# Seeding the fifth product's bank with the common term, in a kernel that sums a long convolution and a feed-forward block

## The chip, the cores and the metric

The kernel runs on one core of a Trainium2 chip. The metric is the device time of one execution in microseconds; several executions are timed and the median is given. A core has five engines that run their own instruction streams and wait for one another through semaphores: TensorE (PE; its weight loads are listed as PEld), VectorE (DVE), ScalarE (ACT), GpSimd (POOL) and SyncE (SP, which here only issues transfers). Matmuls write PSUM, eight banks of 128 partitions x 512 float32; VectorE and ScalarE move results from there.

## The reference

```python
def _A_ref(q, k, v, shift_k, ssm_k, ssm_D):          # S = 2048 tokens, D = 576 channels
    ...                                              # k_shift: causal depthwise conv of k, 4 taps
    kv = k_shift * v
    ...                                              # y: causal depthwise conv of kv with ssm_k, length 2048, by FFT
    y = y + kv * ssm_D[None, None, :]
    return q * y

def _B_ref(x, w1, w2):                               # w1 is 576 x 4608, w2 is 4608 x 576
    h = jnp.einsum("bsd,df->bsf", x, w1)
    h = jnp.maximum(h, zero)
    return jnp.einsum("bsf,fd->bsd", h, w2)

x = A_q
xn = _layernorm(x, axis=-1)
return x + _A_ref(xn, A_k, A_v, A_shift_k, A_ssm_k, A_ssm_D) + _B_ref(xn, B_w1, B_w2)
```

All numbers are float32. The first part (the convolution) and the second part (the feed-forward block) are independent until the last sum.

## The kernel before

**Split operands.** To keep float32 accuracy at the rate of the rounded type (fp32r), every matmul operand is split into a high part (a ScalarE copy) and a low part (the rest). A product of two operands is three matmuls: high x high, high x low, low x high.

**The feed-forward block.** The 2048 tokens go in two halves of 1024, and each half in two blocks of 512 (`b0`, `b1`). The 4608 hidden columns go in 18 chunks of 256, that is two tiles of 128 (`f` = 0, 1). So there are 36 pairs of a half and a chunk, numbered `g`. The first three (`PLAIN`) run plainly (`classical`, line 597). The other 33 run in `quad` (line 629). There the 2 x 2 arrangement of token blocks and of hidden tiles, with the contraction of 512 channels halved too, is multiplied with seven products in place of eight (the scheme of Strassen and Winograd). The sums of operands stand ready: `s1` to `s4` of the tokens, `sums` of the weights. The last 64 channels are added by `rest` (line 583): 2 matmuls. A `product` (line 574) is 6 matmuls of 512 columns: two contraction chunks of three.

**The banks of a quad.** Two PSUM banks carry the hidden results. `bank` (line 560) gives the two alternately, so a new bank waits until every reader of the one before it in the same place is done. In the order of the code, one quad does:

1. Bank 1 (`x`) gets the product of `wa` and `00`. ScalarE copies it, negated, into bank 2 (`y`, line 649). `x` then gets the product with `01` and the rest: it is the first result (block 0, tile 0).
2. `y` gets the product of `wb` and `s2`. It now holds the (negated) common term of the two other results. ScalarE copies it to SBUF (`u2`, line 664).
3. Bank 5 (`x` again) starts anew with the product of `wc` and `s1`. ScalarE copies that to SBUF (`p5`, line 670).
4. `y` gets the product of `wb` and `s3`; bank 5 gets the rest of block 0 and the product of `wd` and `s4`. VectorE adds `u2` to it (line 685): this is the second row's result (block 0, tile 1).
5. ScalarE copies `y`, negated, into bank 4 (line 687). `y` gets the rest of block 1, and VectorE adds `p5` (line 692): block 1, tile 1.
6. Bank 4 gets the product of `wc` and `11` and the rest: block 1, tile 0.

Each result goes through `hidden` (line 588). ScalarE takes the relu (`hh`, line 592) and VectorE the low part (`ll`, line 594).

**The second layer.** Between the products stand eight units of the quad before (`mm2`, line 725; in `quad` they are the calls `unit(0)` to `unit(7)`). A unit is one token tile of 128: 12 matmuls of 288 columns into a pair of banks. VectorE adds the pair to the accumulator (`acc`, line 751). In one stage of the convolution two units a quad are seeded with the accumulator by ScalarE (line 723) and copied back by ScalarE (line 744).

**The weights.** ScalarE makes the high part of a weight (line 513) and GpSimd the low part (line 514), from tiles that GpSimd's queue loads (lines 495 to 506). VectorE makes the sums of the weights (line 526).

**The convolution.** It is a Python generator, `conv` (line 783), whose steps are issued between the matmuls of the feed-forward block. After each product, rest and unit the code calls `tick` (line 1179) with the cost of what was just issued. `tick` issues up to two steps of the generator as long as the convolution lags behind its share. A step that needs a wide bank on loan (it yields "wide") is issued only where `place` is true. In a product, `tick` is called after the first three matmuls and after all six, and only the second call may place a wide step. The stages are: the other half's operands, the filter's transform (lines 916 to 931), taps, gate and transform of the input (lines 936 to 982), products of the spectra with a join and the way back (lines 1041 to 1076), and the last transform with the gate by `x` (lines 1123 to 1167).

**What sets the order.** All matmuls are chained in the order of the code (`tc.issue_after(done["pe"].ins)`). On the other engines, a planner orders instructions by modelled times (`schedule_with_timeline_sim=True`, line 1311). It is bound by data, by `issue_after` and, where both are ready, by the order of the code. The steps of the convolution stand behind the last accumulator addition on VectorE and behind the last relu or copy-back on ScalarE (`here`, line 254), and weight splits on ScalarE behind the latter too.

Of the kernel before, what the change touches and what calls it, by code (L numbers as in the profile page):

```python
# [10 lines left out]
F32 = mybir.dt.float32  # L11
F32R = mybir.dt.float32r
AF = mybir.ActivationFunctionType
OP = mybir.AluOpType
# [3 lines left out]
P = 128  # L18
# [28 lines left out]
W_MM = 512  # L47
# [52 lines left out]
def h3_ffn_kernel(ctx: ExitStack, tc, x, k, v, shift_k, ssm_k, ssm_D, w1, w2, fwd, inv, mid, out):  # L100
    nc = tc.nc
    x = x[0].rearrange("(p u t) d -> u p t d", u=U, t=T)
# [6 lines left out]
    hp = ctx.enter_context(tc.tile_pool(name="hp", bufs=2))  # L109
# [279 lines left out]
    def need(g, o):  # L389
        while g == PLAIN and o not in ready:  # L390
            post(1)
# [95 lines left out]
    raw1, raw2, wa, wb, wc, wd, wr, w2s, sums_w = ({} for _ in range(9))  # L487
# [56 lines left out]
    def split_c(g):  # L544
        wc[g] = split_sums(g, "wc", slice(2, 4))
# [14 lines left out]
    def bank(g, which, name):  # L560
        banks[g, name] = ps_h.tile([P, 512], F32, tag=f"h{(which + 1 + max(g - PLAIN, 0)) % 2}",
                                   name=f"psh{g}_{name}")
        return banks[g, name]

    def matmuls(ps, seq, start):


        for n, (a, m) in enumerate(seq):
            with tc.issue_after(done["pe"].ins) if "pe" in done and not n else nullcontext():
                last = nc.tensor.matmul(ps, a, m, start=start and n == 0, stop=n == len(seq) - 1,  # L570
                                        skip_group_check=True)
        done["pe"] = last

    def product(ps, w, off, o, start=False, g=None, place=True):

        need(g, o)
        for c in range(2):
            h, l = w[:, 0, off + c, :], w[:, 1, off + c, :]
            hi, lo = xo[o][:, 0, c, :], xo[o][:, 1, c, :]
            matmuls(ps, ((h, hi), (h, lo), (l, hi)), start and c == 0)  # L580
            tick(3 * W_MM, place and c == 1)

    def rest(ps, g, b, f):
        need(g, b)
        matmuls(ps, [(wr[g][:, n, 0, f * P:(f + 1) * P], hl[b]) for n in range(2)], False)
        tick(2 * W_MM)

    def hidden(g, b, f, ps):
        k = dict(bufs=2 - (b or f))
        hh = hp.tile([P, 512], F32R, tag=f"hh{b}{f}", name=f"hh{g}_{b}_{f}", **k)  # L590
        ll = hp.tile([P, 512], F32R, tag=f"ll{b}{f}", name=f"ll{g}_{b}_{f}", **k)
        done["act"] = nc.scalar.activation(hh, ps, AF.Relu)  # L592
        with tc.issue_after(done["centred"].ins):
            nc.vector.scalar_tensor_tensor(ll, ps, 0.0, hh, op0=OP.max, op1=OP.subtract)  # L594
        hid[g, b, f] = (hh, ll)
# [33 lines left out]
    def quad(g, units):  # L629


        def unit(n):
            if n + 1 < len(units):
                open_unit(*units[n + 1], n + 1 in stage["seeded"] and more)
            mm2(*units[n])
            post(1)

        def later(o):
            if g == NQ - 1:
                (load_operand if isinstance(o, str) else load_rest_operand)(o)  # L640

        b0, b1 = (0, 1) if g < NQ else (2, 3)
        more = g + 1 < QUADS
        x = bank(g, 0, "1")
        y = bank(g, 1, "2")
        open_unit(*units[0])
        product(x, wa[g], 0, "00", start=True, g=g, place=False)
        later("00")
        nc.scalar.activation(y, x, AF.Copy, scale=-1.0)  # L649
        unit(0)  # L650
        split_c(g)
        unit(1)
        product(x, wa[g], 2, "01", g=g)
        later("01")
        rest(x, g, b0, 0)
        hidden(g, 0, 0, x)
        unit(2)
        split_w2(g, 0)
        if more:
            load_w2(g + 1, 0)  # L660
        product(y, wb[g], 0, "s2", g=g)
        later("s2")
        u2 = hp.tile([P, 512], F32, tag="u2", name=f"u2_{g}", bufs=1)
        nc.scalar.activation(u2, y, AF.Copy)
        unit(3)
        x = bank(g, 0, "5")
        product(x, wc[g], 2, "s1", start=True, g=g)
        later("s1")
        p5 = hp.tile([P, 512], F32, tag="p5", name=f"p5_{g}", bufs=1)
        nc.scalar.activation(p5, x, AF.Copy)  # L670
        if more:
            split_a(g + 1)
        unit(4)
        product(y, wb[g], 2, "s3", g=g)
        later("s3")
        if more:
            sums(g + 1)
        split_w2(g, 1)
        if more:
            load_w2(g + 1, 1)  # L680
        rest(x, g, b0, 1)
        later(2)
        product(x, wd[g], 0, "s4", g=g, place=False)
        later("s4")
        nc.vector.tensor_tensor(u2, x, u2, OP.add)  # L685
        x = bank(g, 0, "4")
        nc.scalar.activation(x, y, AF.Copy, scale=-1.0)  # L687
        hidden(g, 0, 1, u2)
        unit(5)
        unit(6)  # L690
        rest(y, g, b1, 1)
        nc.vector.tensor_tensor(p5, y, p5, OP.add)  # L692
        hidden(g, 1, 1, p5)
        if more:
            split_b(g + 1)
            split_d(g + 1)
            split_r(g + 1)
            if g + 2 < QUADS:
                load_w1(g + 2)
        unit(7)  # L700
        product(x, wc[g], 0, "11", g=g)
        later("11")
        rest(x, g, b1, 0)
        later(3)
        hidden(g, 1, 0, x)

    def token(g, b, i):
        return (g // NQ) * HT + b * BT + i
# [6 lines left out]
    def open_unit(g, b, i, seed=False):  # L715

        t = token(g, b, i)
        slot["open"] = 1 - slot["open"]
        ps = ps_o.tile([P, 2, 512], F32, tag=f"o{slot['open']}", name=f"pso{g}_{t}")
        open_ps[g, t] = ps, slot["open"]  # L720
        if seed and slot["open"] not in unwritten:
            seeded.add(t)
            nc.scalar.activation(ps[:, :, :NH], two(acc[t]), AF.Copy)

    def mm2(g, b, i):
        t = token(g, b, i)
        end = g == QUADS - 1
        if end:
            while t not in added:
                next(stream)  # L730
        cols = slice(i * P, (i + 1) * P)
        ps, slot["closed"] = open_ps.pop((g, t))
        unwritten.discard(slot["closed"])
        slot["units"] += 1
        for h in range(2):
            dc = slice(h * NH, (h + 1) * NH)
            seq = []
            for f in range(FT):
                hh, ll = hid[g, b, f]
                for a, m in ((hh, 0), (hh, 1), (ll, 0)):  # L740
                    seq.append((a[:, cols], w2s[g, f][:, m, dc]))
            matmuls(ps[:, h, :NH], seq, t not in seeded)
        if t in seeded:
            done["act"] = nc.scalar.activation(two(acc[t]), ps[:, :, :NH], AF.Copy)
            seeded.remove(t)
        elif g < PLAIN:
            done["acc"] = nc.vector.scalar_tensor_tensor(two(acc[t]), ps[:, :, :NH],
                                                         rstd[:, t:t + 1], two(acc[t]),
                                                         op0=OP.mult, op1=OP.add)
        else:  # L750
            done["acc"] = nc.vector.tensor_tensor(two(acc[t]), ps[:, :, :NH], two(acc[t]), OP.add)  # L751
        tick(W_UNIT, False)
        if g == NQ - 1 and t % 2:
            nc.sync.dma_start(fin[t // 2], pairs[t - 1])
            load_acc(t - 1 + HT)
        if end:
            if b == 1 and i >= BT - 2:
                move(acc[t], out, t, store=True, queues=(nc.sync, nc.scalar))
            elif t % 2:
                move(pairs[t - 1], out, slice(t - 1, t + 1), store=True)  # L760
# [418 lines left out]
    def tick(cost, place=True):  # L1179

        if clock["done"] or clock["ffn"] < clock["until"]:
            clock["ffn"] += cost
            return
        clock["ffn"] += cost
        clock["conv"] += rate * cost
        steps = 2
        while steps and clock["conv"] >= 0 and (
                not clock["wide"] or place and slot["units"] > slot["lent"]):
            clock["wide"] = False
            try:  # L1190
                c = next(stream)
            except StopIteration:
                clock["done"] = True
                return
            if c == "wide":
                clock["wide"] = True
            elif c < 0:
                clock["until"], clock["conv"] = clock["ffn"] - c, 0.0
                return
            else:  # L1200
                clock["conv"] -= c
                steps -= 1
# [112 lines left out]
```

## Time and profile before

| what | value |
|---|---|
| median of 3 timed runs | 1027.84 us (1026.72 to 1027.87) |
| the profiled execution's own time | 1031.08 us |
| its span, first to last instruction | 1029.3 us |
| mean granted TensorE clock | 0.996 |
| busy: PE, PEld | 1013.8 us (98%), 847.0 us (82%) |
| busy: DVE, ACT, POOL | 711.9 us (69%), 429.7 us (42%), 487.2 us (47%) |
| chain of work that ended last | PE 88%, DVE 4%, DMA 4%, ACT 2%, issue 1% |

Busy shares are means over stages that differ. A matmul's end is modelled, so a busy TensorE can hide small waits. A line of the profile such as "L570 PE MATMUL psh<-x,wa" names the source line, the engine, the operation, and the tile written and those read. Since all matmuls of the feed-forward block are issued by one helper (line 570), they are told apart by tiles: `psh` with `wa`, `wb`, `wc`, `wd` are products of a quad, `psh` with `hl` and `wr` is a rest, `pso` is a unit of the second layer. Matmuls of the convolution are of line 764 (`psf`, `psg`). The name `area` is the convolution's workspace, and `u` and `p` are `u2` and `p5`.

### The profile page before, as it was taken

How to read it: one execution, taken by the hardware profiler on the slowest of the kernel's cores; microseconds unless marked ns; L12 is line 12 of the kernel's file. 1: busy time of each engine (PE TensorE's matmuls, PEld its weight loads, DVE VectorE, ACT ScalarE, POOL GpSimd, SP SyncE). 2: the span in 40 equal slices, each digit the busy share in tenths (PEclk: the TensorE clock that was granted, in tenths of full speed). 3: DMA queues.
4: the chain of work that ended last, by engine and by line, in shares of the span. 5: the costliest groups of instructions: out<-in, count | busy, mean ns of one | idle time of the engine just before them, and what ended most of it. 6: DMA issues, size and time to landing. Idle time of an engine off the chain costs nothing.

```text
span 1029.3 us, 17379 instructions
## 1 busy us (share of the span) xinstructions
PE 1013.8 (98%) x6506; PEld 847.0 (82%) x6506; DVE 711.9 (69%) x1075; ACT 429.7 (42%) x761; POOL 487.2 (47%) x532
## 2 busy tenths in 40 slices
PE   9999999999999999999999999989999999999997
PEld 5898999899988889888888888867767777788777
DVE  5787677776466567879887989455657676556765
ACT  7244334444344444444444444534535454332220
POOL 4335447658444556545555455314423344344450
PEclk9999999999999999999999999989999999999999
DMA  6114367746145564369853433686778888857784
GB/s 169 51 48 119 115 172 163 232 168 183 50 133 174 179 192 147 107 203 371 268 164 125 132 121 109 193 226 201 230 225 240 242 254 241 217 191 243 210 257 116
DMA packets 92249, 184.70 MB, mean 179 GB/s; under 512 B 32082, under 2 KB 44500, under 8 KB 91268
## 3 DMA queue, kind: packets, MB, share of 16 engines
q1 hardware_dynamic: 73588, 123.47, 39.8%
q0 software_dynamic: 18256, 59.22, 19.9%
q8 instruction: 51, 0.84, 0.3%
q10 hardware_dynamic: 320, 0.88, 0.3%
q14 instruction: 34, 0.28, 0.1%
HBM read 119.04 MB, written 45.61 MB: 160 GB/s over the span
## 4 chain that ended last, share of the span: by engine, by line
PE 88%; DVE 4%; DMA 4%; ACT 2%; issue 1%; SPq 0%; POOL 0%; DVEq 0%; ACTq 0%; POOLq 0%
PE pso L570 40%; PE psh L570 34%; PE psf L764 5%; PE psg L764 4%; PE psh_c L570 3%; PE psw L1222 1%; DMA zk<-area 1%; DMA area<-area 1%; DMA r<-in_w 1%; DMA ops<-area 1%; DMA zx<-area 1%; DVE area L943 1%; DVE sums L526 1%; DVE area L944 0%; DVE area L1050 0%
## 5 line engine op out<-in xcount | busy, mean ns | idle before, releaser
L570 PE MATMUL pso<-w,hh 128*128 128x288 f32 x2304 | 468.6, 297 | 0.2 <-DVE area L848 0.2
L570 PEld LDWEIGHTS pso<-w,hh 128*128 128x128 f32 x2304 | 378.5, 188 | 35.3 <-issue 15.6
L570 PE MATMUL pso<-w,ll 128*128 128x288 f32 x1152 | 340.1, 295 | 0.0
L751 DVE TENSOR_TENSOR acc<-pso,acc 128x576 f32<-128x576 f32 x243 | 182.9, 754 | 149.3 <-PE pso L570 148.8
L570 PEld LDWEIGHTS pso<-w,ll 128*128 128x128 f32 x1152 | 216.8, 188 | 0.0
L514 POOL TENSOR_TENSOR wb<-sums,wb 128x512 fp32r<-128x512 f32 x33 | 51.2, 1552 | 229.6 <-ACT wb L513 179.9
L514 POOL TENSOR_TENSOR w<-r,w 128x576 fp32r<-128x576 f32 x72 | 108.9, 1521 | 107.3 <-ACT w L513 107.2
L570 PE MATMUL psh<-x,wa 128*128 128x512 f32 x396 | 102.7, 395 | 1.4 <-ACT psh L649 1.2
L570 PE MATMUL psh<-xs,wb 128*128 128x512 f32 x396 | 102.1, 393 | 0.0
L570 PE MATMUL psh<-hl,wr 128*128 128x512 f32 x264 | 86.0, 407 | 6.3 <-ACT psh L687 6.3
L570 PEld LDWEIGHTS psh<-x,wa 128*128 128x128 f32 x396 | 72.4, 188 | 16.9 <-ACT psh L649 2.1
L570 PEld LDWEIGHTS psh<-xs,wb 128*128 128x128 f32 x396 | 70.8, 188 | 11.4
L514 POOL TENSOR_TENSOR wa<-r,wa 128x512 fp32r<-128x512 f32 x36 | 52.6, 1462 | 53.0 <-ACT wa L513 50.6
L594 DVE SCALAR_TENSOR_TENSOR ll<-psh,hh 128x512 fp32r<-128x512 f32 x66 | 45.2, 685 | 42.9 <-ACT hh L592 42.7
L687 ACT ACTIVATE psh<-psh 128x512 f32<-128x512 f32 x33 | 19.2, 582 | 125.6 <-DVE u L685 125.6
L570 PEld LDWEIGHTS psh<-hl,wr 128*128 128x128 f32 x264 | 46.1, 189 | 27.1 <-issue 13.2
L764 PE MATMUL psf<-area 64*64 64x512 f32 (+10 forms) x592 | 61.2, 473 | 0.0
L592 ACT ACTIVATE hh<-psh 128x512 fp32r<-128x512 f32 x66 | 39.4, 597 | 49.5 <-PE psh L570 48.9
L764 PE MATMUL psg<-area 64*64 64x512 f32 (+10 forms) x568 | 55.3, 453 | 0.0
L592 ACT ACTIVATE hh<-p 128x512 fp32r<-128x512 f32 x33 | 20.9, 633 | 79.3 <-DVE p L692 40.0
L1023 ACT ACTIVATE area<-psg 128x1024 f32<-128x1024 f32 x34 | 33.2, 1025 | 48.8 <-PE psg L764 48.2
L570 PE MATMUL psh<-x,wc 128*128 128x512 f32 x198 | 52.3, 400 | 0.0
(140 smaller groups left out, 1522.6 us busy)
## 6 DMA issues: line engine op xcount, KB each, us to landing
r<-in_w POOLq DMA_DIRECT2D x70, 288.0 KB, 3.4
area<-area SPq DMA_DIRECT2D x144, 128.0 KB, 4.1
r<-in_w POOLq DMA_DIRECT2D x35, 512.0 KB, 5.1
zk<-area SPq DMA_DIRECT2D x64, 144.0 KB, 2.5
area<-zk SPq DMA_DIRECT2D x18, 512.0 KB, 4.6
area<-zx SPq DMA_DIRECT2D x18, 512.0 KB, 4.2
zy<-area SPq DMA_DIRECT2D x18, 512.0 KB, 5.3
area<-zy SPq DMA_DIRECT2D x32, 288.0 KB, 4.9
```

The lines of the kernel that those rows point to most:

```text
L514: nc.gpsimd.tensor_tensor(w[:, 1, :n], src, w[:, 0, :n], OP.subtract)
L526: nc.vector.tensor_tensor(t[:, to], a, b, OP.add)
L570: last = nc.tensor.matmul(ps, a, m, start=start and n == 0, stop=n == len(seq) - 1, skip_group_check=True)
L592: done["act"] = nc.scalar.activation(hh, ps, AF.Relu)
L594: nc.vector.scalar_tensor_tensor(ll, ps, 0.0, hh, op0=OP.max, op1=OP.subtract)
L687: nc.scalar.activation(x, y, AF.Copy, scale=-1.0)
L751: done["acc"] = nc.vector.tensor_tensor(two(acc[t]), ps[:, :, :NH], two(acc[t]), OP.add)
L764: done["pe"] = nc.tensor.matmul(ps, a, m, start=start, stop=stop, skip_group_check=True)
L943: nc.vector.tensor_tensor(e, win[t - n], sk[:, n, :], OP.mult)
L1023: nc.scalar.activation(dst, src, AF.Copy)
L1222: last = nc.tensor.matmul(idle[0], warm[:, :P], warm, start=True, stop=True)
```

## The change

The common term is copied by ScalarE into the fifth product's bank before that product, beside the copy to `u2`. The fifth product accumulates on it. `p5` is now the bank minus `u2`, on VectorE (it was a ScalarE copy). After the rest and the product with `s4`, the bank is the whole second row: ScalarE copies it to `u2`, and VectorE's addition goes. Then ScalarE makes bank 4 as before.

Also, `product` and `rest` take a callback `then`. It issues the evacuation (a copy, subtraction, addition or `hidden`) right after the last matmul and before that place's `tick`, so ahead of the steps of the convolution that `tick` issues. `rest` takes a `place` too, which no call sets.

```diff
@@ -571,19 +571,23 @@
                                         skip_group_check=True)
         done["pe"] = last
 
-    def product(ps, w, off, o, start=False, g=None, place=True):
+    def product(ps, w, off, o, start=False, g=None, place=True, then=None):
 
         need(g, o)
         for c in range(2):
             h, l = w[:, 0, off + c, :], w[:, 1, off + c, :]
             hi, lo = xo[o][:, 0, c, :], xo[o][:, 1, c, :]
             matmuls(ps, ((h, hi), (h, lo), (l, hi)), start and c == 0)
+            if c and then:
+                then()
             tick(3 * W_MM, place and c == 1)
 
-    def rest(ps, g, b, f):
+    def rest(ps, g, b, f, place=True, then=None):
         need(g, b)
         matmuls(ps, [(wr[g][:, n, 0, f * P:(f + 1) * P], hl[b]) for n in range(2)], False)
-        tick(2 * W_MM)
+        if then:
+            then()
+        tick(2 * W_MM, place)
 
     def hidden(g, b, f, ps):
         k = dict(bufs=2 - (b or f))
@@ -644,30 +648,35 @@
         x = bank(g, 0, "1")
         y = bank(g, 1, "2")
         open_unit(*units[0])
-        product(x, wa[g], 0, "00", start=True, g=g, place=False)
+        product(x, wa[g], 0, "00", start=True, g=g, place=False,
+                then=lambda: nc.scalar.activation(y, x, AF.Copy, scale=-1.0))
         later("00")
-        nc.scalar.activation(y, x, AF.Copy, scale=-1.0)
         unit(0)
         split_c(g)
         unit(1)
         product(x, wa[g], 2, "01", g=g)
         later("01")
-        rest(x, g, b0, 0)
-        hidden(g, 0, 0, x)
+        rest(x, g, b0, 0, then=lambda: hidden(g, 0, 0, x))
         unit(2)
         split_w2(g, 0)
         if more:
             load_w2(g + 1, 0)
-        product(y, wb[g], 0, "s2", g=g)
+        u2 = hp.tile([P, 512], F32, tag="u2", name=f"u2_{g}", bufs=1)
+
+        def common():
+            fifth.append(bank(g, 0, "5"))
+            nc.scalar.activation(fifth[0], y, AF.Copy)
+            nc.scalar.activation(u2, y, AF.Copy)
+
+        fifth = []
+        product(y, wb[g], 0, "s2", g=g, then=common)
         later("s2")
-        u2 = hp.tile([P, 512], F32, tag="u2", name=f"u2_{g}", bufs=1)
-        nc.scalar.activation(u2, y, AF.Copy)
         unit(3)
-        x = bank(g, 0, "5")
-        product(x, wc[g], 2, "s1", start=True, g=g)
+        x = fifth[0]
+        p5 = hp.tile([P, 512], F32, tag="p5", name=f"p5_{g}", bufs=1)
+        product(x, wc[g], 2, "s1", g=g,
+                then=lambda: nc.vector.tensor_tensor(p5, x, u2, OP.subtract))
         later("s1")
-        p5 = hp.tile([P, 512], F32, tag="p5", name=f"p5_{g}", bufs=1)
-        nc.scalar.activation(p5, x, AF.Copy)
         if more:
             split_a(g + 1)
         unit(4)
@@ -680,17 +689,25 @@
             load_w2(g + 1, 1)
         rest(x, g, b0, 1)
         later(2)
-        product(x, wd[g], 0, "s4", g=g, place=False)
+        fourth = []
+
+        def second_row():
+            nc.scalar.activation(u2, x, AF.Copy)
+            fourth.append(bank(g, 0, "4"))
+            nc.scalar.activation(fourth[0], y, AF.Copy, scale=-1.0)
+            hidden(g, 0, 1, u2)
+
+        product(x, wd[g], 0, "s4", g=g, place=False, then=second_row)
         later("s4")
-        nc.vector.tensor_tensor(u2, x, u2, OP.add)
-        x = bank(g, 0, "4")
-        nc.scalar.activation(x, y, AF.Copy, scale=-1.0)
-        hidden(g, 0, 1, u2)
         unit(5)
         unit(6)
-        rest(y, g, b1, 1)
-        nc.vector.tensor_tensor(p5, y, p5, OP.add)
-        hidden(g, 1, 1, p5)
+
+        def last_tile():
+            nc.vector.tensor_tensor(p5, y, p5, OP.add)
+            hidden(g, 1, 1, p5)
+
+        rest(y, g, b1, 1, then=last_tile)
+        x = fourth[0]
         if more:
             split_b(g + 1)
             split_d(g + 1)
@@ -700,9 +717,8 @@
         unit(7)
         product(x, wc[g], 0, "11", g=g)
         later("11")
-        rest(x, g, b1, 0)
+        rest(x, g, b1, 0, then=lambda: hidden(g, 1, 0, x))
         later(3)
-        hidden(g, 1, 0, x)
 
     def token(g, b, i):
         return (g // NQ) * HT + b * BT + i
```

## The prediction

> **What bounds the kernel now.** I read the page first, then TensorE's own waits, the order of time around the longest of them, the groups by shape, and the stretches by granted clock.
>
> ```profile
> span 1029.3 us, 17379 instructions
> PE 1013.8 (98%) x6506; PEld 847.0 (82%) x6506; DVE 711.9 (69%) x1075; ACT 429.7 (42%) x761; POOL 487.2 (47%) x532
> PEclk9999999999999999999999999989999999999999
> ```
>
> TensorE is the bound: it is busy 98% of the span, and the change takes no matmul away and adds none. What can move is TensorE's idle time and its clock. One of 40 slices shows a lower digit for the clock. The waits of TensorE (who waited for whom: us in total, times, longest):
>
> ```profile
> PE psh L570 <- ACT psh L687: 6.3, 3, 2.7
> PE psh L570 <- ACT psh L649: 1.2, 1, 1.2
> PE psw L1222 <- DVE warm L1205: 1.2, 1, 1.2
> ```
>
> The first two are waits for copies between banks that this change moves; the third is of the start, which it does not touch, and all that follow are shorter. So the prize among the waits is 7.5 us. The longest of the three L687 waits, in order of time (start, duration, what, and in brackets the idle time before it):
>
> ```profile
> 683.51 1.29 DVE L1062 SCALAR_TENSOR_TENSOR area<-area,sign 128x1024 f32<-128x1024 f32 x1 [2.06 <-DMA area<-area]
> 685.97 2.48 DVE L1050 TENSOR_TENSOR area<-psf,area 128x512 f32<-128x512 f32 x4 [0.84 <-DMA area<-area]
> 686.74 0.29 PE L570 MATMUL pso<-w,ll 128*128 128x288 f32 x1
> 688.37 0.68 DVE L685 TENSOR_TENSOR u<-psh,u 128x512 f32<-128x512 f32 x1
> 689.09 0.58 ACT L687 ACTIVATE psh<-psh 128x512 f32<-128x512 f32 x1 [4.52 <-DVE u L685]
> 689.72 1.22 PE L570 MATMUL psh<-hl,wr 128*128 128x512 f32 x2 [2.69 <-ACT psh L687]
> ...
> 522.03 0.73 PE L570 MATMUL psh<-hl,wr 128*128 128x512 f32 x2 [1.44 <-ACT psh L687]
> 758.02 0.74 PE L570 MATMUL psh<-hl,wr 128*128 128x512 f32 x2 [2.14 <-ACT psh L687]
> ```
>
> VectorE was held by the convolution (a join and four products, both waiting for DMA); behind them stood the addition of the second row (L685), behind that ScalarE's copy into the fourth product's bank (L687), and behind that TensorE. After the longest wait the clock fell:
>
> ```profile
> 689.70:695.90 6.20, 6.18 (x20) 5.50 (x21) 3.33 (x6) 2.27 (x5) 1.05 (x1) 0.50 0.73 199
> 695.90:700.00 4.10, 4.10 (x27) 3.73 (x26) 1.03 (x2) 1.70 (x3) 3.90 (x6) 1.00 0.00 0
> ```
>
> (stretch, us, then busy time of PE, PEld, DVE, ACT, POOL, then the granted clock). For 6.2 us TensorE ran dense at 0.50: that work takes 3.1 us at 1.00, so the drop cost 3.1 us. The waits of 2.14 and 1.44 us left the clock up. The Trainium skill ("TensorE: Matmul & The Clock Gate", Part 1) says that the clock halves after an idle window of about 3.4 us. The trace differs, since 2.69 us sufficed; if that wait did not cause the drop, the credit of 3.1 us would fall away and the sum below be 1025.7; I follow the trace.
>
> **The change part by part.** Prices by group (line, engine, shapes, count, then busy us, mean ns of one, and idle time before):
>
> ```profile
> L685 DVE TENSOR_TENSOR u<-psh,u 128x512 f32<-128x512 f32 x33 | 22.7, 688 | 33.0 <-PE psh L570 32.8
> L670 ACT ACTIVATE p<-psh 128x512 f32<-128x512 f32 x33 | 19.7, 596 | 45.0 <-PE psh L570 44.7
> L664 ACT ACTIVATE u<-psh 128x512 f32<-128x512 f32 x33 | 19.5, 592 | 11.8 <-PE psh L570 11.7
> L687 ACT ACTIVATE psh<-psh 128x512 f32<-128x512 f32 x33 | 19.2, 582 | 125.6 <-DVE u L685 125.6
> ```
>
> *Instructions.* Each of the 33 chunks loses one VectorE addition (L685, 0.69 us) and gains one VectorE subtraction of the same shape for p5 (no row of its own; L685 is the nearest, same operands, so 0.69 us): nothing for VectorE. ScalarE loses the copy of L670 (0.60), gains the copy into the fifth bank (as L687, 0.58) and the copy of the finished second row (as L664, 0.59): 0.57 us more a chunk, 19 us in all, from 42% to 44% busy. That is hidden by ScalarE's idle time. No DMA is added or taken away. The callbacks move evacuations ahead of the convolution's steps, so on VectorE and ScalarE the steps, and on SyncE's and GpSimd's queues the DMAs that they issue, go behind an evacuation that waits for TensorE.
>
> *The second row.* Now the fourth bank's copy waits for VectorE; then it stands behind one ScalarE copy only. For the cover I need the length of a unit:
>
> ```profile
> 1011.30 12.76 PE pso L570 x96
> ```
>
> This is from the chain of waits: 12.76/96 = 0.133 us a matmul, 1.59 us a unit of 12. Two units lie between the fourth product's operand s4 and the matmuls that overwrite y: 3.19 us. Two copies (0.59 + 0.58), some 0.25 us after the product (929.35 to 929.61 below), are over at 1.4 us, so ScalarE may be 1.8 us late before TensorE waits. In the stall shown ScalarE had been idle for 4.52 us before L687. Removed: all 6.3 us (the bounds are 0, if ScalarE were as late as VectorE is, and 6.3), and with it the 3.1 us of half clock.
>
> *The copy L649*, at its one wait:
>
> ```profile
> 185.04 0.63 ACT L468 ACTIVATE area<-area 128x512 fp32r<-128x512 f32 x1 [3.27 <-DMA ops<-area]
> 186.10 0.58 ACT L649 ACTIVATE psh<-psh 128x512 f32<-128x512 f32 x1
> 186.72 1.65 PE L570 MATMUL psh<-x,wa 128*128 128x512 f32 x6 [1.22 <-ACT psh L649]
> ```
>
> A convolution copy that waited for DMA stood ahead of it. The callback puts L649 ahead of what is issued at the second half of the product, not at the first half. Between 0 and 1.2 I take the middle, 0.6.
>
> *The new wait.* The fifth product used to start a fresh bank and waited for no copy; now it accumulates on the copied common term. The nearest rows are L664's, whose place the copy takes, in a quiet chunk and in a late one:
>
> ```profile
> 927.97 1.55 PE L570 MATMUL psh<-xs,wb 128*128 128x512 f32 x6
> 929.35 0.42 PE L570 MATMUL pso<-w,hh 128*128 128x288 f32 x2
> 929.61 0.60 ACT L664 ACTIVATE u<-psh 128x512 f32<-128x512 f32 x1 [1.29 <-PE psh L570]
> 930.94 1.55 PE L570 MATMUL psh<-xs,wc 128*128 128x512 f32 x6
> ...
> 217.07 0.63 ACT L513 ACTIVATE wa<-r 128x512 fp32r<-128x512 f32 x1 [1.46 <-DMA r<-in_w]
> 217.50 1.54 PE L570 MATMUL psh<-xs,wc 128*128 128x512 f32 x6
> 217.60 0.58 ACT L664 ACTIVATE u<-psh 128x512 f32<-128x512 f32 x1
> ...
> ACT wa L513 <- DMA r<-in_w: 12.0, 8, 2.6
> ACT u L664 <- PE psh L570: 11.7, 13, 1.3
> ```
>
> In the quiet chunk the copy ends at 930.21, 0.73 us before the fifth product: the unit between hides it. In the late one a weight split that waits for its load stands ahead, although the source has it later (the planner moved it), and the copy ends at 218.18: with the 0.05 us from the copy's end to the next matmul (689.67 to 689.72 above), a stall of 0.73 us. Behind the waiting copy stand the copy to u2, the next accumulator seed and the splits; u2 has until y is written again, a unit and a product later. Bounds: 0 (TensorE does not wait there today, so there is nothing to gain), and 8 x 0.73 = 5.8 us if each of the 8 waits for a load fell on it. L664 waited for TensorE itself in 13 chunks; in the other 20 ScalarE was busy until then, mostly, as its rows of 0.6 us suggest, for less than the slack. Nearest is the quiet case: I take 1.0.
>
> *p5 on VectorE.* Its subtraction must read the fifth bank before the remainder is added there, a unit and a product later: 1.59 + 1.38 (927.97 to 929.35 above) = 2.97 us. Needed are 0.25 + 0.69, so VectorE may be 2.0 us late. Bounds: 0, and the three old stalls carried over to here. Their chain is shorter by a ScalarE copy with its 0.05 us (0.63) and the cover by 0.22: 2.3 + 1.0 + 1.7 = 5.0 us. But the subtraction is ahead of the convolution group that is issued at its own product, where L685 stood behind everything. I take 0.5.
>
> **Sum.** The profiled execution took 1031.08 us, 1.8 more than its span: 1031.08 - 6.3 - 3.1 - 0.6 + 1.0 + 0.5 = 1022.6. The timed median is 1027.84, 3.24 lower. If the timed runs lacked the half clock (3.1 us, which nearly is the difference), 1022.6 stands for them too; if the difference is the profiler's, it is 1027.84 - 8.5 = 1019.3. The first accounts for the number without a further assumption, so I forecast **1022 us**.
>
> **The rivals.**
>
> *The stalls change places.* VectorE is as late at the p5 subtraction as it was at L685. For it: the join and the products held VectorE until 688.4 above. Against it: the new order. Then 5.0 of 6.3 us stay: 1027.84 - 1.3 - 0.6 + 1.0 = 1026.9, no difference.
>
> *The fifth product waits for its seed.* The upper bound, 5.8 instead of 1.0: 1026.8, no difference. For it speaks the split ahead of L664, against it the 0.73 us of slack.
>
> *Slower: VectorE starves the convolution.* The first row gives the chunk's length (first and last start of 33: 897.5/32 = 28.0 us), the second the stretch in which VectorE computes the taps:
>
> ```profile
> L664 ACT ACTIVATE u<-psh x33: 573/597/606, 94.4 to 991.9; 128x512 f32<-128x512 f32 x33
> 396.00:640.00 244.00, 242.49 (x1568) 212.64 (x1567) 205.88 (x271) 111.12 (x200) 130.59 (x129) 1.00 0.54 172
> L943 DVE TENSOR_TENSOR area<-area 128x576 f32<-128x576 f32 x48 | 46.0, 959 | 0.2
> L592 ACT ACTIVATE hh<-psh 128x512 fp32r<-128x512 f32 x66 | 39.4, 597 | 49.5 <-PE psh L570 48.9
> ```
>
> VectorE is idle for 38.1 of 244 us; that is 8.7 chunks, so 4.4 us a chunk. The callbacks put evacuations that wait for TensorE, and for the relu of 0.60 us, ahead of taps that filled that time. If five places in a chunk each idle by one tap (0.96) and 0.2 us, 5.8 us a chunk, VectorE becomes the bound and lags by 1.4 x 8.7 = 12 us, which TensorE meets at the next transform: 1022 + 12 = 1034. The turn is where the lag eats the gain of 5.8 us, at 4.4 + 5.8/8.7 = 5.1 us a chunk. For it: VectorE is 84% busy there. Against it: where VectorE is behind, it finds TensorE's product done and waits for nothing. The Trainium skill ("TensorE: Matmul & The Clock Gate", Architectural detail) has it that ScalarE and VectorE run strictly first in, first out, which is what makes a waiting evacuation hold up the steps; the rows above, where L685 stands behind the join, agree.
>
> *It does not do what it says:* the planner orders the engines by modelled times, as the moved split shows, and may undo the new order; the second row's independence of VectorE stays, so part of the gain does.
>
> **How the numbers follow.** Forecast 0.60; stalls that change places 0.12; the seed's wait 0.11; starved convolution 0.14; planner otherwise 0.03, put with the forecast. Below 0.2% (2.1 us) a measurement of this kernel can hardly tell a change from none: faster is below 1025.8, slower above 1029.9. So faster 0.63, same 0.22, slower 0.15. Low end: every stall and the half clock credited against the median, 1027.84 - 10.6 = 1017. High end: 1030, which takes in both cases of no difference and leaves out the starved one. The forecast's own range is 1018 to 1025.
>
> **What would show it.** Right: TensorE waits no more for the fourth bank's copy, the clock row has 9 in all 40 slices, ScalarE is at 44%. The new wait shows as TensorE waiting for the ScalarE copy into psh before the matmuls with xs and wc, 1 us in total; p5 as VectorE holding the remainder's matmuls. Wrong: several us in either, VectorE under 15 us idle between 396 and 640, waits of the transforms' matmuls (L764) for VectorE, or a clock drop at a new place.

## The result, and the profile after

The changed kernel is slower: 1040.74 us median of 4 runs (1033.38 to 1041.89) against 1027.28 us (1026.12 to 1027.87, 4 runs), a ratio of 1.0114 with a 95% interval of 1.0089 to 1.0139. The prediction was 1022 us, with a range up to 1030. The profiled execution took 1041.72 us. The head of the page of the changed kernel:

```profile
span 1039.9 us, 17380 instructions
PE 1017.8 (98%) x6506; PEld 848.5 (82%) x6506; DVE 701.1 (67%) x1075; ACT 443.6 (43%) x794; POOL 478.6 (46%) x532
PEclk9999999999999999998989999999999999999999
```

VectorE has less to do and ScalarE more, TensorE the same number of matmuls, yet the span is 10.6 us longer, and two slices have a lower clock in place of one. TensorE's waits in the changed kernel (who waited for whom: us in total, times, longest):

```profile
PE psh L570 <- DVE p L678: 7.1, 3, 3.8
PE pso L570 <- DVE acc L767: 2.2, 2, 1.7
PE psh L570 <- ACT psh L652: 1.8, 3, 1.1
PE psh L570 <- ACT psh L668: 1.8, 3, 0.9
PE psw L1238 <- DVE warm L1221: 1.2, 1, 1.2
PE psg L780 <- ACT area L938: 0.6, 1, 0.6
```

The waits for the fourth bank's copy (6.3 us before) are gone. At the head now stands a wait for p5's subtraction (line 678), which TensorE meets at the remainder added after it. The second line, the accumulator addition, is also new. Line 652 is the old line 649; line 668 is the seed of the fifth bank.

**Where p5 was late.** The order of time in the changed kernel around the first and the longest of the three waits (start, duration, what, and in brackets the idle time before it):

```profile
462.92 1.55 PE L570 MATMUL psh<-xs,wb 128*128 128x512 f32 x6
464.70 0.76 DVE L526 TENSOR_TENSOR sums<-r 128x256 f32<-128x256 f32 x2 [4.76 <-DMA r<-in_w]
466.05 1.50 DVE L526 TENSOR_TENSOR sums<-sums,r 128x256 f32<-128x256 f32 x1
467.47 1.95 DVE L959 TENSOR_TENSOR area<-area 128x576 f32<-128x576 f32 x1
469.34 0.68 DVE L678 TENSOR_TENSOR p<-psh,u 128x512 f32<-128x512 f32 x1
470.07 1.22 PE L570 MATMUL psh<-hl,wr 128*128 128x512 f32 x2 [3.06 <-DVE p L678]
...
519.84 1.55 PE L570 MATMUL psh<-xs,wc 128*128 128x512 f32 x6
521.75 0.76 DVE L526 TENSOR_TENSOR sums<-r 128x256 f32<-128x256 f32 x2 [2.98 <-DMA r<-in_w]
523.10 1.52 DVE L526 TENSOR_TENSOR sums<-sums,r 128x256 f32<-128x256 f32 x1
527.41 0.68 DVE L678 TENSOR_TENSOR p<-psh,u 128x512 f32<-128x512 f32 x1
528.15 1.22 PE L570 MATMUL psh<-hl,wr 128*128 128x512 f32 x2 [3.79 <-DVE p L678]
```

In the second of them the fifth product is over at 521.2 (its start, 519.84, and six matmuls of 0.23), and p5's operand is ready. VectorE first waits for the next chunk's weights to land, then sums them, computes taps between the sums, and comes to p5 6.2 us later. In the code the sums stand after p5, one product further down. The planner put them ahead. Line 530 binds the sums only to the last accumulator addition that VectorE made; in the stage of the taps, units 3 and 4 are seeded and copied back by ScalarE, so that addition is unit 2's, and the sums are free to go early. In the other stages the binding addition itself comes after p5 and the order of the code holds.

The kernel before had the same early sums in the same chunk, as its order of time shows:

```profile
461.63 0.76 DVE L526 TENSOR_TENSOR sums<-r 128x256 f32<-128x256 f32 x2 [3.55 <-DMA r<-in_w]
462.16 0.58 ACT L670 ACTIVATE p<-psh 128x512 f32<-128x512 f32 x1
464.42 0.73 PE L570 MATMUL psh<-hl,wr 128*128 128x512 f32 x2
```

VectorE waited there 3.55 us for the load, and nobody minded: p5 was copied by ScalarE, and the remainder followed without a wait.

**The second row.** Its stall came back one step later. The order of time of the changed kernel at the place of the longest old wait:

```profile
698.55 1.28 DVE L1078 SCALAR_TENSOR_TENSOR area<-area,sign 128x1024 f32<-128x1024 f32 x1 [2.07 <-DMA area<-area]
701.01 2.48 DVE L1066 TENSOR_TENSOR area<-psf,area 128x512 f32<-128x512 f32 x4 [0.84 <-DMA area<-area]
703.41 0.75 DVE L767 TENSOR_TENSOR acc<-pso,acc 128x576 f32<-128x576 f32 x1
704.22 0.54 PE L570 MATMUL pso<-w,hh 128*128 128x288 f32 x2 [1.68 <-DVE acc L767]
```

The same join and the same four products hold VectorE. ScalarE now makes the fourth bank without it, and TensorE can do the last remainder (line 570, 0.62 us). But the next unit then needs a pair of banks that the late accumulator addition has not yet read: 1.68 us of idle time where there were 2.69.

**The clock.** The two stretches of lower clock in the changed kernel (stretch, us, then busy time of PE, PEld, DVE, ACT, POOL, then the granted clock):

```profile
468.45:475.28 6.83, 5.21 (x15) 4.43 (x16) 2.57 (x4) 1.36 (x3) 1.92 (x4) 0.50 1.02 407
526.48:533.31 6.83, 5.16 (x15) 4.38 (x16) 3.80 (x7) 1.31 (x3) 0.25 (x1) 0.50 0.45 130
```

Both begin inside a wait for p5. TensorE's work in them, 5.21 and 5.16 us at 0.50, would have taken half: 5.2 us are lost, against 3.1 in the profile before.

**The account of the two profiled executions**, in us: p5 +7.1; half clock 5.2 - 3.1 = +2.1; second row -6.3; accumulator addition +2.2; seed +1.8; first copy 1.8 - 1.2 = +0.6; the convolution's matmuls +2.0 (the distance from the start of one to the start of the next, summed over the 1104 places where two follow each other, is 78.8 us before and 80.8 after; 1.0 of it are two waits of these matmuls for ScalarE). That is 9.5 of the 10.6. The medians differ by more, 13.5 us, since the profiled execution before was 3.8 above its median and the one after 1.0 above its own.

### The profile page after: what moved, and what is told of

Same layout as the page of the kernel before. It is cut to its first block, busy times and chain, and to the rows that moved or that the text cites. A ratio compares the mean times of both kernels' runs of the same rounds, so it can differ in the third digit from the quotient of the medians.

```text
span 1039.9 us, 17380 instructions
## 1 busy us (share of the span) xinstructions
PE 1017.8 (98%) x6506; PEld 848.5 (82%) x6506; DVE 701.1 (67%) x1075; ACT 443.6 (43%) x794; POOL 478.6 (46%) x532
## 4 chain that ended last, share of the span: by engine, by line
PE 77%; DVE 6%; DMA 6%; issue 5%; POOL 3%; ACT 1%; SPq 0%; POOLq 0%; DVEq 0%; ACTq 0%
PE pso L570 36%; PE psh L570 30%; PE psf L780 5%; PE psg L780 4%; DMA r<-in_w 4%; PE psh_c L570 3%; DVE area L959 1%; POOL wc L514 1%; DVE acc L767 1%; DMA acc<-in_x 1%; DMA ops<-area 1%; DMA area<-area 1%; POOL wd L514 1%; POOL wr L514 1%; DVE ll L598 1%
## 5 line engine op out<-in xcount | busy, mean ns | idle before, releaser
L514 POOL TENSOR_TENSOR w<-r,w 128x576 fp32r<-128x576 f32 x72 | 106.8, 1492 | 98.9 <-ACT w L513 98.7
L695 ACT ACTIVATE u<-psh 128x512 f32<-128x512 f32 x33 | 19.7, 598 | 121.6 <-PE psh L570 103.7
L570 PE MATMUL psh<-xs,wc 128*128 128x512 f32 x198 | 51.7, 396 | 1.9 <-ACT psh L668 1.8
L570 PE MATMUL psh<-xs,wd 128*128 128x512 f32 x198 | 53.5, 408 | 0.0
```

Of the source, the lines that this page charges most:

```text
L514: nc.gpsimd.tensor_tensor(w[:, 1, :n], src, w[:, 0, :n], OP.subtract)
L695: nc.scalar.activation(u2, x, AF.Copy)
```

## The experiments

The theory: p5's place on VectorE behind the early sums is the loss (7.1 us and the half clock that comes with it). Rivals: the new order of the evacuations is the loss, since it changes when everything else is issued; or the seed in the fifth bank. Kernels that were run together share their runs of the kernel before; ratios are to these.

### The change again, and three ways to take it apart

**after_again**, the changed kernel as it is:

> The kernel after, unchanged, beside the others on the same chip. Theory 1: 1033 to 1042 us, TensorE's waits for p5 between 5 and 9 us in the same chunks (the 15th to the 21st quad, where taps are computed); where fewer of them are over about 2.5 us, less half clock and a shorter time. If the stalls came by chance, they would stand in other chunks.

Measured: 1039.12 us (1035.8 to 1039.64), ratio 1.0112 (1.0096 to 1.0129). The loss repeats. Its waits for p5 are 6.2 us in all, the longest 4.33.

**sums_behind**, the changed kernel with the sums bound behind p5:

```diff
-        with at_sums(g):
+        with at_sums(g), tc.issue_after(done["p5"].ins) if "p5" in done else nullcontext():
...
-                then=lambda: nc.vector.tensor_tensor(p5, x, u2, OP.subtract))
+                then=lambda: done.update(p5=nc.vector.tensor_tensor(p5, x, u2, OP.subtract)))
```

> The kernel after, with one edge more: the weight sums of the next chunk (L526) are issued on VectorE behind the subtraction that makes p5. Nothing else is changed. Theory 1 (in the stage of the taps the planner put the sums, which wait for a weight load, ahead of the p5 subtraction, and TensorE waits for that): TensorE's waits for p5 fall from 7.1 us to under 1 us, both stretches of half clock (13.7 us, worth 6.8 us) go, and the time is 1041 - 7.1 - 6.8, about 1027 us (1024 to 1029). Rival (VectorE is overfull in that stage whatever the order): the waits change their name but stay above 5 us, time 1036 us or more.

Measured: 1029.02 us (1027.87 to 1030.89), ratio 1.0012 (1.0003 to 1.0022), granted clock 1.00. Its waits of TensorE:

```profile
PE psh L570 <- ACT psh L668: 2.4, 4, 1.1
PE pso L570 <- DVE acc L767: 2.2, 2, 1.7
PE psh L570 <- ACT psh L652: 1.4, 3, 0.6
```

No wait for p5 is left, and no half clock between start and end. One binding takes back 10.1 us against after_again: the theory holds for that part. But the kernel is still not faster than before (the median lies at the top of the range expected), so something else eats the gain.

**common_only**, the changed kernel's data flow with the evacuations issued after the steps of the convolution, as before:

```diff
+            tick(3 * W_MM, place and c == 1)
             if c and then:
                 then()
-            tick(3 * W_MM, place and c == 1)
...
+        tick(2 * W_MM, place)
         if then:
             then()
-        tick(2 * W_MM, place)
```

> The common term goes into the fifth bank and p5 is a subtraction as in the kernel after, but every evacuation is issued behind the convolution's steps, as before the change. Theory 1: the loss comes with this half of the change, so the time is that of the kernel after, 1033 to 1042 us, with TensorE waiting for p5 on VectorE for about 7 us. Rival 2 (the callbacks, which put evacuations ahead of the convolution's steps, cause the loss): about 1027 us.

Measured: 1031.86 us (1028.57 to 1036.37), ratio 1.0039 (1.002 to 1.0058). Its waits for p5 are 2.4 us (three, longest 1.5), its accumulator wait 1.7, its seed 1.4. So p5 is late in this order as well, but less. The time lies between what the theory and the rival had forecast. The runs scatter over 8 us, and the profiled one (1030.06 us) is among the quicker. The trace says what sets the size in one place: in the chunk at about 462 us p5 starts 4.6 to 4.7 us after the first sum in all three executions (469.34 - 464.70 = 4.64 above; 4.66 here; 4.65 in after_again), and the first sum starts when the weights have landed: 3.37 us after the end of the fifth product in the changed kernel's profile, 1.17 here, 1.32 in after_again. The later the landing, the longer TensorE waits there: 3.06, 1.55 and 1.68 us. Why the loads land at other times was not tried.

**callbacks_only**, the kernel before with its own evacuations issued ahead of the steps:

```diff
+            if c and then:
+                then()
             tick(3 * W_MM, place and c == 1)
...
+        product(y, wb[g], 0, "s2", g=g, then=lambda: nc.scalar.activation(u2, y, AF.Copy))
...
+        product(x, wc[g], 2, "s1", start=True, g=g,
+                then=lambda: nc.scalar.activation(p5, x, AF.Copy))
...
+            nc.vector.tensor_tensor(u2, x, u2, OP.add)
```

> The data flow of the kernel before (fresh fifth bank, p5 by a ScalarE copy, VectorE's addition for the second row), with every evacuation issued ahead of the convolution's steps. Theory 1: no loss, and little gain, since the planner's order changes for only 8 of 1077 VectorE instructions: 1024 to 1029 us. Rival 2 (the callbacks cause the loss): 1035 us or more.

Measured: 1031.09 us (1028.04 to 1034.64), ratio 1.0035 (1.0019 to 1.005). This was a miss: the order alone costs 3.6 us. The second row's waits fell only from 6.3 to 4.7 us, and the time between the convolution's matmuls rose from 78.8 to 81.5 us. The two halves of the change, common_only and callbacks_only, cost 0.0039 and 0.0035 alone and 0.0112 together. So they make each other worse; by what, beyond the time of landing, was not settled.

### The disputed cost by itself

**p5_on_vector**, the kernel before with one line changed:

```diff
-        nc.scalar.activation(p5, x, AF.Copy)
+        nc.vector.tensor_copy(p5, x)
```

> The kernel before with one instruction changed: p5 is copied out of the fresh fifth bank by VectorE (L670) and no longer by ScalarE. No seed, no callbacks, the second row as before. The planner puts the weight sums ahead of it in the tap stage, as in the kernel after. Theory 1 (it is p5 on VectorE behind the sums that costs): TensorE waits for this copy 2 to 6 us in the 15th to 21st quad, beside the old 5 to 6 us for the second row, and the time is 1030 to 1036 us. Rival (the seeded bank or the second row on ScalarE costs): no wait for the copy, about 1027.5 us.

Measured: 1034.96 us (1032.99 to 1039.96), ratio 1.0073 (1.0044 to 1.0103). Its waits of TensorE:

```profile
PE psh L570 <- DVE p L670: 6.3, 4, 3.1
PE psh L570 <- ACT psh L687: 4.2, 2, 2.7
```

With neither the seed nor the new order, a copy of the same shape on VectorE brings the p5 wait (6.3 us) and makes the kernel 7.9 us slower. The sums stand ahead of it again, as the order of time shows:

```profile
461.47 0.76 DVE L526 TENSOR_TENSOR sums<-r 128x256 f32<-128x256 f32 x2 [4.03 <-DMA r<-in_w]
466.11 0.68 DVE L670 COPY p<-psh 128x512 f32<-128x512 f32 x1
466.85 0.73 PE L570 MATMUL psh<-hl,wr 128*128 128x512 f32 x2 [3.06 <-DVE p L670]
```

The profile also holds three stretches of half clock, 13.65 us together, and its execution (1038.34 us) is one of the slower ones. This run shows that p5 on VectorE suffices for the loss, and sums_behind that the sums ahead of it are what makes p5 late.

### Without the new order

**sums_behind_no_callbacks**, the data flow of the change, the sums behind p5, the evacuations after the steps (both diffs above together):

> The data flow of the kernel after with the sums of the weights issued behind the p5 subtraction, and without the callbacks: evacuations behind the convolution's steps, as before the change. Theory 1 (the callbacks cost some 2 us in the convolution's own matmuls, 80.7 against 78.8 us there, because a filter copy on ScalarE goes behind an evacuation): 1029.0 - 2, about 1027 us (1026 to 1028). Rival (the callbacks shorten the waits by more than they cost): 1029 us or more.

Measured: 1025.8 us (1025.23 to 1028.11), ratio 0.9987 (0.9977 to 0.9997). No wait for p5; the accumulator addition 3.1, the seed 1.8, the first copy 1.1. Against sums_behind, the order of the evacuations costs 1.0012 - 0.9987, some 2.6 us (the two were not run together, so by their ratios).

**sums_and_split_behind_no_callbacks**, the same, and the next chunk's weight split on ScalarE bound behind the copies of the common term:

```diff
-        split_a(g + 1)
+        with tc.issue_after(done["u2"].ins):
+            split_a(g + 1)
```

> As the run above, and the next chunk's weight split (wa, L513) is issued on ScalarE behind the copies into the fifth bank and u2. Theory 1 (what is left of the new wait, TensorE for the seed of the fifth bank, 2.4 us, comes from this split ahead of the seed in two of its four places): that wait falls to about 1 us and the time is 1 us shorter than the run above, about 1026 us. Rival (the seed is late for another reason): no difference.

Measured: 1024.31 us (1024.06 to 1026.46), ratio 0.9974 (0.9961 to 0.9988). The seed's wait is not in its trace (0.6 us of it is in the trace of the second run, best_again below), and the first copy's is 0.6. In two of the seed's four places in the run above (0.15 and 0.47 us) the split that waited for its load stood ahead of the copies. In the third (0.43 us) the seed of an accumulator did, waiting for VectorE, and that is the wait left in best_again. In the fourth (0.70 us) a late VectorE had not yet read the bank. So the binding explains only a part. This kernel is faster than the one before and than the changed one; against the run above the intervals overlap.

**scalar_row**, the kernel before, with the second row freed of VectorE in another way: ScalarE copies the fifth bank to SBUF, and VectorE adds `u2` there. There is no seed, and p5 stays on ScalarE.

```diff
-        nc.vector.tensor_tensor(u2, x, u2, OP.add)
+        row2 = hp.tile([P, 512], F32, tag="ll01", name=f"row2_{g}", bufs=1)
+        nc.scalar.activation(row2, x, AF.Copy)
         x = bank(g, 0, "4")
         nc.scalar.activation(x, y, AF.Copy, scale=-1.0)
+        nc.vector.tensor_tensor(u2, row2, u2, OP.add)
```

> The kernel before with one ScalarE copy more: after the product with s4 ScalarE copies the fifth bank to SBUF, and VectorE adds u2 to that copy (both operands in SBUF). The fifth bank starts fresh, p5 stays a ScalarE copy, there are no callbacks. So neither bank waits for VectorE. Theory 1 (the second row's wait for VectorE was worth its 6.3 us, and what ate it in the kernel after was p5): TensorE's waits for the fourth bank go, some 2 us come back as a wait for a late accumulator addition, and the time is 1022 to 1025 us. Rival (the 6.3 us come back elsewhere in the same chunks whatever is done): 1027 us.

Measured: 1027.21 us (1026.36 to 1029.29), ratio 1.0002 (0.9992 to 1.0011). Its first two waits of TensorE:

```profile
PE pso L570 <- DVE acc L753: 4.8, 3, 2.3
PE psh L570 <- ACT psh L649: 1.9, 2, 1.4
```

The fourth bank's wait is gone, and nothing is gained: the rival held. Of 6.3 us, 4.8 come back as the wait for VectorE's accumulator addition: the fourth bank was only the first thing that a late VectorE held up.

### Which half of the order costs, and can the late addition be avoided

These four were run together. **best_again** is the fastest kernel unchanged:

> The same kernel as the fastest so far, unchanged, on the chip of the three others: 1024.3 us the first time, so 1023.5 to 1025.5 us if that was the kernel and not the chip; 1026 us or more if it was chance.

Measured: 1024.85 us (1023.77 to 1027.3), ratio 0.9976 (0.9964 to 0.9987). It repeats.

**best_product_callbacks** issues the evacuations behind the products ahead of the steps, **best_rest_callbacks** those behind the remainders (the relu and low part of three of the four tiles, and the last addition). Their diffs, in this order:

```diff
             if c and then:
                 then()
+            tick(3 * W_MM, place and c == 1)
...
         if then:
             then()
+        tick(2 * W_MM, place)
```

(each with the same call taken away above the callback).

> The same order, with the evacuations behind the weight products (the seeds, the fifth product's subtraction, the second row) issued ahead of the convolution's steps, those behind the remainders after them. All callbacks together cost 2 to 3 us here (1029.0 against 1025.8 us, with the sums behind in both). If the loss comes from ScalarE's evacuations of the remainders, which wait for TensorE ahead of the convolution's filter copies, this one stays at 1024 to 1025 us. Rival: it comes from the evacuations behind the products: 1026 to 1027 us.

> The other half: only the evacuations behind the remainders (relu of the hidden tiles, the last addition) are issued ahead of the convolution's steps. If these carry the loss of the callbacks: 1026 to 1027 us, with the wait of a transform's matmul for the filter copy (0.6 us) in the trace and some 2 us more between the convolution's matmuls. Rival: 1024 to 1025 us, and the loss is with the products.

Measured: 1025.61 us (1023.19 to 1026.69), ratio 0.9983 (0.997 to 0.9996), for the products; 1028.72 us (1027.56 to 1030.32), ratio 1.0018 (1.0007 to 1.0029), for the remainders. The loss is with the remainders: 3.9 us against best_again, and 0.8 for the products, whose intervals overlap. The waits of TensorE in best_rest_callbacks that best_again does not have:

```profile
PE psf L781 <- issue: 1.1, 1, 1.1
PE psg L781 <- ACT acc L761: 0.8, 1, 0.8
PE psg L781 <- ACT area L939: 0.6, 1, 0.6
```

All three are matmuls of the convolution, and the time between its matmuls, which takes in such waits, is 81.7 us here, 79.2 in best_again and in best_product_callbacks. The order of time on ScalarE before the third of these waits, in best_rest_callbacks:

```profile
305.03 0.63 ACT L596 ACTIVATE hh<-p 128x512 fp32r<-128x512 f32 x1 [5.13 <-PE pso L570]
305.56 0.51 ACT L863 ACTIVATE area<-psf 128x432 f32<-128x432 f32 x1
305.97 0.52 ACT L863 ACTIVATE area<-psg 128x432 f32<-128x432 f32 x1
307.52 0.69 ACT L939 ACTIVATE area<-area 128x288 f32<-128x288 f32 x1
308.26 0.71 PE L781 MATMUL psg<-area 64*64 64x288 f32 x8 [0.62 <-ACT area L939]
```

And the same place in best_again:

```profile
301.74 0.53 ACT L863 ACTIVATE area<-psf 128x432 f32<-128x432 f32 x1 [2.75 <-PE psf L781]
302.49 0.53 ACT L863 ACTIVATE area<-psg 128x432 f32<-128x432 f32 x1 [0.22 <-PE psg L781]
304.11 0.63 ACT L596 ACTIVATE hh<-p 128x512 fp32r<-128x512 f32 x1 [1.09 <-PE pso L570]
305.78 0.70 ACT L939 ACTIVATE area<-area 128x288 f32<-128x288 f32 x1
```

With the relu of block 1, tile 1 ahead, ScalarE idles 5.13 us, and two copies of the convolution (line 863) come after it, not in the gap before it. They push back the filter copy (line 939), for which the matmul waits 0.62 us. The two other waits have other causes. Before the one of 0.8 us stands a weight split that waited 4.25 us for its load, and behind it the copy-back of an accumulator (line 761). The one of 1.1 us has its like at the same place in best_product_callbacks (0.91 us) and best_no_wide_second_rest (0.84), whose intervals overlap with that of best_again. So the runs show that the remainders' evacuations cost the 3.9 us, but the trace puts only 0.6 us down to a relu; where the rest arises was not settled.

**best_no_wide_second_rest** keeps the wide convolution step out of the second remainder:

```diff
-        rest(x, g, b0, 1)
+        rest(x, g, b0, 1, place=False)
```

> The order without callbacks, with the next chunk's weight sums behind the fifth product's subtraction and its weight split behind the ScalarE copies (1024.3 us when it was run), and the wide convolution step kept out of the second remainder. What is left there of TensorE's waits is the one for VectorE's accumulator addition, 2.5 us in all, 1.7 us of it behind a join and four products of the convolution issued at that remainder. If the step's place is the cause, that wait falls under 1 us and the time is about 1022.5 us. Rival: the steps only go to another place and VectorE is late there: 1024 us or more, with a new wait for VectorE or ScalarE of 1 to 2 us.

Measured: 1025.44 us (1023.99 to 1027.28), ratio 0.9979 (0.9967 to 0.9991): no gain over best_again. The wait for the accumulator addition in the stage of the joins is still there, 1.83 us (1.68 in best_again), behind the same join and four products; only the shorter one later (0.79 us) went. The expectation was wrong: keeping the step out of that remainder does not move what holds VectorE there. The wait remains open to a better schedule.

## Why the prediction was wrong

- **p5 on VectorE** is the step that failed. I took 0.5 with bounds of 0 and 5.0; it measured 7.1 us in the profile, 6.2 in the repeat, with 5.2 us lost at half clock behind it in the first. My reason was that "the subtraction is ahead of the convolution group that is issued at its own product". That is true and was not the question: I asked what the *code* issues ahead of it, and only among the convolution's steps. The planner had moved the weight sums there, with a DMA wait of their own, and I had seen it move a split in the same way on ScalarE. In the profile before, the wait of L526 stood in front of L670 at the same place (3.55 us); it cost nothing, so it was not in any list of TensorE's waits. The bound was wrong for the same reason: it was made from the second row's stalls, and these are from another stage and another cause.
- **The rival of stalls that change places** named the right engine and the right victim, but the wrong thing ahead of p5 (the join and the products) and so too low a price: 5.0 us. At the joins, where I expected it, p5 was in time.
- **The second row**: TensorE waits no more for the fourth bank, as forecast. But I credited the whole 6.3 us, and the lower bound that I named, 0, concerned ScalarE alone. What is late next is VectorE's accumulator addition: 2.2 us came back in the changed kernel, 4.8 in scalar_row.
- **The half clock**: 3.1 us were credited; 5.2 were lost. My reading that the timed runs lacked it falls too. Profiles without a drop between start and end have a mean granted clock of 0.998 to 1.000; of the 25 timed runs of the kernel before beside after_again 14 are below that, the median run (1027.54 us, 0.997) among them. So the median run most likely had a drop already, and by my own second reading the sum would have been 1019.3, further off still. The clock is not all of the loss either: the one timed run of the changed kernel at 0.999, 1033.38 us, is 6.1 us above the median before.
- **L649**: I took 0.6 of gain; its waits rose from 1.2 to 1.8 us in the profile. **The seed**: 1.0 predicted, 1.8 measured (2.4 in sums_behind), in the changed kernel for the reason given, the split ahead of it, in all three places. Both terms are small and mis-sized, and L649's has the wrong sign.
- **The order of the evacuations** had a price in a rival, on VectorE (12 us). VectorE did not become the bound: between 396 and 640 us it is idle for 53.0 us in the changed kernel, against 38.1 before and the 15 that I named as a sign. The cost, 2.6 to 3.9 us, comes from the evacuations behind the remainders. I had priced them on VectorE alone; the one wait that the trace puts down to them (0.6 us) is for ScalarE.
- **Instructions**: ScalarE is at 43%, predicted 44%; the work added on it is hidden, as predicted.

The direction of the forecast was right for the data flow alone. With the sums and the split put back behind the evacuations, and without the new order, it gains 2.5 us (0.0024 of 1027; 1.3 to 3.7 by the interval), less than half of the 5.8 forecast. Whether the two bindings alone would gain something in the kernel before was not run.

## What to carry to other kernels

Before moving an evacuation to another engine, list what that engine executes just ahead of that point in the trace, above all instructions that wait for a DMA; a stall there is invisible while nobody stands behind it. Where a planner orders the engines, the order of the code isn't an argument: bind prefetch work behind the evacuation explicitly. And when a late engine is taken out of one chain, ask for which of its results TensorE waits next before crediting the wait.

## What the runs showed of the hardware

The clock does not fall after every long wait, and the traces show where it does. In each trace the granted clock changes only at multiples of 3.41 us from one another: in the changed kernel it is low from 468.45 to 475.28 us and from 526.48 to 533.31, each 2 x 3.41 us, with 51.2 us or 15 x 3.41 between. Cut by this grid, two stretches of callbacks_only around its longest wait, and then two of best_no_wide_second_rest (same columns as above):

```profile
686.29:689.70 3.41, 2.52 (x19) 2.29 (x18) 2.57 (x6) 0.04 (x1) 0.00 (x0) 1.00 0.90 247
689.71:693.12 3.41, 1.63 (x11) 1.54 (x12) 2.89 (x5) 1.11 (x2) 0.00 (x0) 1.00 1.05 352
```

```profile
686.22:689.63 3.41, 1.58 (x10) 1.15 (x9) 3.41 (x6) 0.05 (x1) 0.00 (x0) 1.00 0.98 380
689.64:693.04 3.40, 3.40 (x14) 3.28 (x14) 2.11 (x4) 0.78 (x2) 0.00 (x0) 0.50 1.01 274
```

In callbacks_only a wait of 2.68 us, at the same place as in the kernel before, fell across an edge, 0.89 us on one side and 1.78 on the other: the clock stayed at 1.00. In the other kernel a wait of 1.83 us lay within one stretch, and the clock fell at its end. All 14 traces agree, their first 20 us and their ends left out. Each of the nine drops follows a stretch in which TensorE was idle for 1.83 us or more in all; the most idle stretch that no drop follows is the one with 1.78 us. A drop lasted 3.41 us where TensorE was busy all through it (five drops; some 1.7 us lost), and 6.83 us where it was idle for another 0.60 us or more in the first half (four drops; 2.6 to 3.1 us lost in the three of the kernels before and after). So where a wait lies against the grid decides as well as its length, and as an order of instructions does not fix that, a term for the clock should be given as a chance. The Trainium skill ("TensorE: Matmul & The Clock Gate", Part 1) speaks of an idle window of about 3.4 us; the stretches here have that length, but 1.83 us of idle time in one was enough.
